# Forget attention and two MLPs: where VectorE and TensorE place the fifth attention unit and two weight packets

## The chip, the cores and the metric

The kernel runs on one core of a Trainium2 chip. The metric is device time in microseconds of one execution; smaller is better. Matrix products run on TensorE, elementwise work on VectorE, ScalarE and GpSimd, and SyncE's queue (SP) issues nearly all transfers. Each engine takes its instructions strictly in the order in which they were written for it.

## The reference

```python
q, k, v: (4, 8, 576, 64); s: (4, 8, 576)
cum = cumsum(maximum(s, 0))
scores = q @ k.T / 8 + minimum(-(cum_i - cum_j), 0), -1e9 above the diagonal
attn = softmax(scores); x = (attn @ v) as (2304, 512)
h = x @ w_in1;  x = (s * relu(h)**2 + b) @ w_out1      # 512 -> 2048 -> 512
h = x @ w_in2;  out = (relu(h) + alpha * min(h, 0)) @ w_out2
```

Inputs and outputs are float32; the weights arrive in a wider form and are converted on the chip.

## The kernel before

**Attention.** The work is cut into 32 units; a unit is a batch, a pair of heads and either the first 320 or the last 256 rows of queries. For each head of a unit, `scores` takes products of q and k on TensorE (L457 in the first eight units, L459 and L460 later), joins them with the gate bias on VectorE (L435 writes the bias, L461 joins and takes the row's extreme), takes exponentials on ScalarE (L473, which also sums the row), adds a small number and inverts the sum on VectorE (L480, L481), and multiplies by it on GpSimd (L484, the normalisation). `values` then transposes the result on TensorE (L515), copies it to SBUF (L519) and multiplies by v (L531); ScalarE copies the outcome into the block of x (L546). `transpose_qk` turns q and k on VectorE (L375). In names such as `sc0_3_0_0_1` the first digits are head and block of rows, the last three the unit. The first four units (numbers 0 to 3, called the early ones) have buffers of their own and run before any MLP work. While they do, TensorE also runs products of zeros that nobody reads (`busy`, L97).

**The MLP.** Tokens go in blocks of 256. A block needs all of its x, split by ScalarE (L130, the rounded part) and VectorE or GpSimd (L131, the rest): `xh` and `xl`, each in four pieces. The hidden layer goes in 16 slices f: `up` (L772, twelve matmuls into `hp`), relu and square on ScalarE (L791, L793), a split into `gh` and `gl` (L130, L131), and `down` (L886, twelve matmuls), which trails `up` by two slices.

**Weight packets.** Slice f of the first layer comes as packet f: two transfers of 512 KB (L208 `wi`, L212 `wo`) into raw tiles, and for each half a ScalarE pass (L140), two VectorE passes (L141, L142, after which the raw tile is free) and a split (L130 on ScalarE; L131 on VectorE for `wi`, on GpSimd for `wo`). The raw tiles are reused in a fixed rotation: packets 3 and 6 share one pair, 4 and 7 another, 5 and 8 a third.

**What sets the order.** The program is written as Python generators that take turns, and a scheduler with a model of the engines then orders each engine's instructions, preferring what was written earlier. `tc.issue_after(ins)` holds everything in its block, on the engine of `ins`, behind `ins`. The fifth unit is number 4 (`EARLY`), the first one without buffers of its own. Before the change, packets 0 to 3 and this unit's turning and first scores were written among the early units, with packet 4 (`AHEAD - 1` = 3, `AHEAD` = 4) written with the first slice:

```python
        yield from alternate(scores(us[2], 1), values(us[1], 1))
        packet(0, 3)
        yield from alternate(scores(us[3], 0), values(us[2], 0), transpose_qk(u))
```

Of the kernel before, what the change touches and what calls it, by code (L numbers as in the profile page):

```python
# [19 lines left out]
def tile_forget_attention__then__two_mlps(  # L20
# [108 lines left out]
    def split(hi, lo, src, lo_eng=nc.vector):  # L129
        nc.scalar.copy(hi, src)  # L130
        lo_eng.tensor_tensor(out=lo, in0=src, in1=hi.bitcast(F32), op=ALU.subtract)  # L131

# [123 lines left out]

    xf = {}

# [110 lines left out]
    def transpose_qk(u):  # L369
# [4 lines left out]
        for dst, src in zip(turned, u.nats):  # L374
            nc.vector.transpose(dst, src)  # L375
        yield
# [27 lines left out]
    def scores(u, h):  # L404
# [11 lines left out]
        for r in u.blocks:  # L416
            i0, i1 = IB[r]
            rows = i1 - i0
            if u.early and r != 1:
                big, col = u.buf(two, 0, F32, "", f"probs{h}{r}"), 0  # L420

            width = -(-i1 // P) * P if i1 < S else S
            pt = probs[r] = big[:, col : col + width]
            col += width
            if width > i1:
                nc.gpsimd.memset(pt[:, i1:], 0.0)
            if r == 0:
                nc.gpsimd.memset(pt[64:P, 0:64], 0.0)

            if flip:  # L430
                nc.scalar.activation(
                    pt[:rows, :i1], u.cums[h][:rows, :i1], AF.Relu, scale=-1.0, bias=cumT[:rows, r, head : head + 1]
                )
            else:
                nc.vector.tensor_scalar(  # L435
                    out=pt[:rows, :i1], in0=u.cums[h][:rows, :i1], scalar1=cumT[:rows, r, head : head + 1],
                    scalar2=0.0, op0=ALU.subtract, op1=ALU.min,
                )
            nc.gpsimd.affine_select(
                out=pt[:rows, i0:i1], in_=pt[:rows, i0:i1], pattern=[[-1, rows]], base=0,  # L440
                channel_multiplier=1, compare_op=ALU.is_ge,
                fill=-MASKED if flip else MASKED,
            )
# [36 lines left out]
        nc.vector.tensor_scalar(out=sm[:, :nr], in0=sm[:, :nr], scalar1=1e-9, scalar2=None, op0=ALU.add)  # L480
        nc.vector.reciprocal(sm[:, :nr], sm[:, :nr])  # L481
        for m, r in enumerate(u.blocks):
# [7 lines left out]
    def values(u, h):  # L490
# [45 lines left out]
        if u.n < EARLY:  # L536
            busy(4 if (u.n, h) == (EARLY - 1, 0) else 1)
        t0 = u.b * S + q0
# [22 lines left out]

    done = 0

    def attention():
# [32 lines left out]
        yield from alternate(scores(us[2], 1), values(us[1], 1))  # L597
        packet(0, 3)
        yield from alternate(scores(us[3], 0), values(us[2], 0), transpose_qk(u))
        yield from alternate(scores(us[3], 1), values(us[2], 1))  # L600
        yield from values(us[3], 0)
        last = us[3]
        for n in range(EARLY, len(units)):
            nxt = Unit(n + 1) if n + 1 < len(units) else None
            if nxt:
                load_qk(nxt)
            yield from alternate(scores(u, 0), values(last, 1))
            done = n
# [21 lines left out]
    def inputs(layer, t):  # L630
# [20 lines left out]
        for c in range(NCC):  # L651
            on_pool = layer == 0 and t
            split(xh[c], xl[c], src[:, c], nc.gpsimd if on_pool else nc.vector)
        return xh, xl
# [314 lines left out]
    while done < reached(0):  # L969
        next(side)  # L970
    for f in range(AHEAD):
        packet(0, f)
    fetch(0, AHEAD + 1)

    x, late = inputs(0, 0), []
    for n in range(len(BLOCKS) * NF):
# [5 lines left out]
        if layer == 0 and t == 0 and f + AHEAD < NF:  # L982
            with tc.issue_after(relus[f - 1]) if f else nullcontext():
                packet(0, f + AHEAD)
            for g in range(f + AHEAD + 1, min(f + AHEAD + 3, NF)):
                fetch(0, g)
# [54 lines left out]
```

## Time and profile before

| | |
|---|---|
| Median of 3 runs | 1041.17 us (1040.21 to 1043.41) |
| Profiled execution, its own time | 1043.1 us |
| Its span, first to last instruction | 1041.2 us |
| TensorE busy | 1021.4 us, 98% of the span |
| VectorE busy | 686.3 us, 66% |
| ScalarE busy | 672.7 us, 65% |
| GpSimd busy | 468.1 us, 45% |
| Mean granted TensorE clock | 0.993 of full speed |

The busy time of an engine counts instructions that do work. TensorE's matmuls overlap, so its busy time is not its peak. "Granted clock" is the share of full speed that the chip gave TensorE.

### The profile page before, as it was taken

Reading aid. Unit: us, or ns where it says so; the run is one execution under the profiler, and the core shown is the slowest. Engines: PE = TensorE matmul, PEld = TensorE weight load, DVE = VectorE, ACT = ScalarE, POOL = GpSimd, SP = SyncE. Lnnn points to the kernel's source line nnn. Section 1 sums busy time; section 2 is a strip of 40 time slices with the busy share of each in tenths; the row PEclk is TensorE's granted clock in tenths of the full one; section 3 lists DMA queues with packets and bytes.
Section 4 is the critical chain, followed back from the end, with each engine's and each line's share of the span. In section 5 each row is a group of like instructions: output and inputs, shape, how many; then the busy total and the mean of one; then the engine's idle time right before and its main releaser. Section 6 shows DMA issues by size and latency. Waiting matters only on the chain.

```text
span 1041.2 us, 20629 instructions
## 1 busy us (share of the span) xinstructions
PE 1021.4 (98%) x6952; PEld 927.0 (89%) x6952; DVE 686.3 (66%) x1605; ACT 672.7 (65%) x1669; POOL 468.1 (45%) x892
## 2 busy tenths in 40 slices
PE   9889999999999999999999999999999999999998
PEld 4568899999999999999999888998799999999996
DVE  6879875687677766667655975767775456446443
ACT  5868866777787877778776776645564455345443
POOL 5546675666677666677562100288721011001000
PEclk9889999999999999999999999999999999999999
DMA  7979533343232432234214762466654235334331
GB/s 157 268 174 252 150 63 69 69 97 72 52 84 62 90 92 52 67 68 93 64 44 145 241 201 81 124 194 200 196 178 143 98 101 179 105 95 132 107 104 55
DMA packets 197929, 125.44 MB, mean 120 GB/s; under 512 B 138496, under 2 KB 167936, under 8 KB 197824
## 3 DMA queue, kind: packets, MB, share of 16 engines
q1 hardware_dynamic: 193744, 123.56, 42.9%
q8 instruction: 55, 0.90, 0.4%
q10 hardware_dynamic: 4080, 0.57, 0.3%
q14 instruction: 50, 0.41, 0.1%
HBM read 106.19 MB, written 17.90 MB: 119 GB/s over the span
## 4 chain that ended last, share of the span: by engine, by line
PE 77%; DMA 5%; POOL 5%; ACT 4%; DVE 4%; issue 3%; SPq 1%; ACTq 0%; DVEq 0%; POOLq 0%
PE hp L772 18%; PE acc L896 16%; PE acc L886 16%; PE p L806 13%; PE pt L515 4%; PE av L531 4%; POOL sum L727 2%; PE sc L460 2%; DMA vn<-in_v_dram 1%; PE sc L459 1%; DMA sums_d<-w 1%; DMA wo<-in_moe_w_out_dram 1%; PE acc_first L97 1%; PE sc L457 1%; POOL probs L484 1%
## 5 line engine op out<-in xcount | busy, mean ns | idle before, releaser
L772 PE MATMUL hp<-xh,w 128*128 128x256 f32 (+1 forms) x1024 | 229.1, 301 | 0.5 <-ACT r L791 0.5
L896 PE MATMUL acc<-w,ring 128*128 128x512 f32 x864 | 214.1, 391 | 0.0
L896 PEld LDWEIGHTS acc<-w,ring 128*128 128x128 f32 x864 | 156.0, 188 | 27.8
L772 PEld LDWEIGHTS hp<-xh,w 128*128 128x128 f32 x1024 | 171.4, 189 | 6.6 <-ACT r L791 1.0
L886 PE MATMUL acc<-gh,w 128*128 128x256 f32 x896 | 172.3, 286 | 0.5 <-ACT res L915 0.3
L772 PE MATMUL hp<-xl,w 128*128 128x256 f32 (+1 forms) x512 | 152.6, 298 | 0.0
L886 PEld LDWEIGHTS acc<-gh,w 128*128 128x128 f32 x896 | 136.0, 189 | 3.1 <-issue 1.6
L872 POOL TENSOR_TENSOR cc<-u,t 128x256 f32<-128x256 f32 x32 | 25.9, 809 | 228.9 <-DVE u L863 198.9
L886 PE MATMUL acc<-gl,w 128*128 128x256 f32 x448 | 118.7, 288 | 2.0 <-POOL gl L131 2.0
L484 POOL TENSOR_SCALAR probs<-probs,sm 64x64 f32<-64x64 f32 (+4 forms) x160 | 91.0, 581 | 64.8 <-DVE sm L481 52.5
L473 ACT ACTIVATE probs<-probs,nm 64x64 f32<-64x64 f32 (+4 forms) x160 | 90.0, 563 | 37.8 <-DVE nm L461 25.7
L131 POOL TENSOR_TENSOR gl<-r,gh 128x256 fp32r<-128x256 f32 x112 | 89.3, 797 | 51.3 <-ACT gh L130 44.8
L806 PE MATMUL p<-xs,sums 128*128 128x256 f32 x768 | 104.4, 282 | 0.7 <-DVE u L848 0.7
L806 PEld LDWEIGHTS p<-xs,sums 128*128 128x128 f32 x768 | 97.8, 189 | 2.8 <-DVE u L848 1.2
L772 PEld LDWEIGHTS hp<-xl,w 128*128 128x128 f32 x512 | 97.1, 190 | 3.3 <-issue 0.4
L461 DVE CUSTOM_DVE_ANT_0 probs<-sc,probs 128x320 f32<-128x320 f32 (+3 forms) x160 | 68.2, 427 | 40.4 <-PE sc L460 28.0
L791 ACT ACTIVATE r<-hp 128x256 f32<-128x256 f32 (+1 forms) x144 | 58.1, 403 | 44.5 <-PE hp L772 36.9
L806 PEld LDWEIGHTS p<-xs,w 128*128 128x128 f32 x576 | 78.8, 189 | 9.0 <-DVE u L863 2.3
L806 PE MATMUL p<-xs,w 128*128 128x256 f32 x576 | 82.2, 283 | 2.4 <-DVE u L863 1.5
L886 PEld LDWEIGHTS acc<-gl,w 128*128 128x128 f32 x448 | 80.1, 189 | 4.8 <-POOL gl L131 2.6
L515 PE MATMUL pt<-ident,probs 128*128 128x128 f32 x480 | 75.0, 277 | 5.7 <-POOL probs L484 5.6
L817 DVE SCALAR_TENSOR_TENSOR ph<-pl,misc,ph 128x512 f32<-128x512 f32 x64 | 52.7, 823 | 38.2 <-ACT pl L833 38.0
(149 smaller groups left out, 2133.9 us busy)
## 6 DMA issues: line engine op xcount, KB each, us to landing
sums<-sums_d SPq DMA_DIRECT2D x128, 256.0 KB, 2.7
wi<-in_moe_w_in_dram SPq DMA_DIRECT2D x32, 512.0 KB, 5.0
wo<-in_moe_w_out_dram SPq DMA_DIRECT2D x32, 512.0 KB, 5.0
cum<-cum_d SPq DMA_DIRECT2D x32, 288.0 KB, 3.8
sums_d<-w SPq DMA_DIRECT2D x64, 128.0 KB, 1.9
cum<-cum_d SPq DMA_DIRECT2D x30, 160.0 KB, 3.2
nat<-in_k_dram SPq DMA_DIRECT2D x64, 72.0 KB, 2.5
x_d<-res SPq DMA_DIRECT2D x18, 256.0 KB, 2.2
```

Source lines behind the costliest of these rows:

```text
L131: lo_eng.tensor_tensor(out=lo, in0=src, in1=hi.bitcast(F32), op=ALU.subtract)
L461: nc.vector.tensor_tensor_reduce(out=pt[:rows, j0:j1], in0=scr, in1=pt[:rows, j0:j1], scale=SCALE if flip else -SCALE, scalar=init, op0=AL ...
L473: nc.scalar.activation(pt[:rows, :n], pt[:rows, :n], AF.Exp, bias=nm[:rows, m : m + 1], scale=1.0 if flip else -1.0, accum_out=sm[:rows, m ...
L484: nc.gpsimd.tensor_scalar(out=probs[r][:rows, :n], in0=probs[r][:rows, :n], scalar1=sm[:rows, m : m + 1], scalar2=1.0, op0=ALU.mult, op1=A ...
L515: nc.tensor.transpose(tp[:, o : o + P], u.probs[h][r][:, k0 : k0 + P], ident)
L531: nc.tensor.matmul(av[:, nq - w : nq], lhs, part[:, o : o + w], start=(c == 0 and z == 0), stop=(c == last_c and z == len(parts) - 1), ski ...
L772: nc.tensor.matmul(hs, a[:, c], b[c], start=(n == 0), stop=(n == len(terms) * NCC - 1))
L791: relus.append(nc.scalar.activation(r, hs, AF.Relu, scale=1.0 / W_SCALE).ins)
L806: nc.tensor.matmul(bank, lhs[:, c * P : (c + 1) * P], rhs[:, c], start=(start and c == 0 and z == 0), stop=(c == 1 and z == 2), skip_group ...
L817: nc.vector.scalar_tensor_tensor(out=r, in0=u, scalar=nalpha[:, f : f + 1], in1=r, op0=ALU.mult, op1=ALU.add).ins
L886: nc.tensor.matmul(banks[d] if count == 2 else acc[d // 2][:, d % 2], a[:, d * P : (d + 1) * P], b, start=(f == 0 and (d % 2 == 0 or count ...
L896: nc.tensor.matmul(banks[m], a[:, m * P : (m + 1) * P], b, start=(f == 0 and b is woh and a is gh), stop=(f == NF - 1 and a is gl),)
```

## The change

The turning and the biases of unit 4 on VectorE are held behind the eighth reciprocal (L481), which is that of the last early head (`turns[2 * EARLY - 1]`). Packet 3 is held behind the fourth `xl` split of the first block, on VectorE (`x_parts[-1]`), and so is packet 4. The last `values` of the early units is written before unit 4's scores, so that the block of x is complete first. Four products of zeros after the first head of unit 3 become one. All arithmetic stays.

```diff
-        return
+    def behind_early(u):
+        return tc.issue_after(turns[2 * EARLY - 1]) if u.n == EARLY else nullcontext()
...
         for dst, src in zip(turned, u.nats):
-            nc.vector.transpose(dst, src)
+            with behind_early(u):
+                nc.vector.transpose(dst, src)
...
-                nc.vector.tensor_scalar(
+                with behind_early(u):
+                    nc.vector.tensor_scalar(
...
-        nc.vector.reciprocal(sm[:, :nr], sm[:, :nr])
+        turns.append(nc.vector.reciprocal(sm[:, :nr], sm[:, :nr]).ins)
...
-            busy(4 if (u.n, h) == (EARLY - 1, 0) else 1)
+            busy(1)
...
-        packet(0, 3)
-        yield from alternate(scores(us[3], 0), values(us[2], 0), transpose_qk(u))
+        yield from alternate(scores(us[3], 0), values(us[2], 0))
         yield from alternate(scores(us[3], 1), values(us[2], 1))
         yield from values(us[3], 0)
+        yield from alternate(values(us[3], 1), transpose_qk(u))
+        done = EARLY
+        yield
...
-            yield from alternate(scores(u, 0), values(last, 1))
+            yield from alternate(scores(u, 0), *([values(last, 1)] if n > EARLY else []))
...
-            split(xh[c], xl[c], src[:, c], nc.gpsimd if on_pool else nc.vector)
+            x_parts.append(split(xh[c], xl[c], src[:, c], nc.gpsimd if on_pool else nc.vector))
...
-    for f in range(AHEAD):
-        packet(0, f)
+    x, late = inputs(0, 0), []
+    with tc.issue_after(x_parts[-1]):
+        packet(0, AHEAD - 1)
     fetch(0, AHEAD + 1)
...
-            with tc.issue_after(relus[f - 1]) if f else nullcontext():
+            with tc.issue_after(relus[f - 1] if f else x_parts[-1]):
                 packet(0, f + AHEAD)
```

On VectorE, before: the sum and the reciprocal of unit 3's second head (`sm_3_0_1`) among packets 3 and 4 (`wt_3`, `wt_4`) and the turning and biases of unit 4 (`turned_0_1`, `probs_0_1_0`).

```order
L470 TENSOR_SCALAR nm_3_0_1_722<-nm_3_0_1_722 128x1
L141 TENSOR_SCALAR wt_4_0_901<-wt_4_0_901 128x512
L131 TENSOR_TENSOR xl_0_870<-xf_433,xh_0_869 128x256
L142 SCALAR_TENSOR_TENSOR wt_4_0_901<-wi_4_272,wt_4_0_901 128x512
L375 STREAM_TRANSPOSE turned_0_1_695<-nat_0_1_564 128x832
L131 TENSOR_TENSOR w_3_0_11_654<-wt_3_0_645,w_3_0_12_653 128x512
L435 TENSOR_SCALAR probs_0_1_0_817<-cum_0_0_1_573,cumT 128x448
L435 TENSOR_SCALAR probs_0_1_0_817<-cum_0_0_1_573,cumT 128x576
L141 TENSOR_SCALAR wt_4_1_905<-wt_4_1_905 128x512
L480 TENSOR_SCALAR sm_3_0_1_723<-sm_3_0_1_723 128x3
L142 SCALAR_TENSOR_TENSOR wt_4_1_905<-wo_4_273,wt_4_1_905 128x512
L481 RECIPROCAL sm_3_0_1_723<-sm_3_0_1_723 128x3
```

The same place in the changed kernel, where lines stand a few numbers later (L472 for L470, L482 for L480, L483 for L481, L376 for L375, L437 for L435):

```order
L472 TENSOR_SCALAR nm_3_0_1_704<-nm_3_0_1_704 128x1
L131 TENSOR_TENSOR xl_0_807<-xf_433,xh_0_806 128x256
L482 TENSOR_SCALAR sm_3_0_1_705<-sm_3_0_1_705 128x3
L483 RECIPROCAL sm_3_0_1_705<-sm_3_0_1_705 128x3
L376 STREAM_TRANSPOSE turned_0_1_794<-nat_0_1_564 128x832
L437 TENSOR_SCALAR probs_0_1_0_889<-cum_0_0_1_573,cumT 128x448
L437 TENSOR_SCALAR probs_0_1_0_889<-cum_0_0_1_573,cumT 128x576
```

The sum and the reciprocal now follow one `xl` split; packets 3 and 4 are gone from here, and the turning and the biases stand behind the reciprocal.

On VectorE in the changed kernel, from the fourth `xl` split on; before, nothing of packets 3 and 4 stood behind that split.

```order
L131 TENSOR_TENSOR xl_0_807<-xf_433,xh_0_806 128x256
L141 TENSOR_SCALAR wt_3_0_816<-wt_3_0_816 128x512
L141 TENSOR_SCALAR wt_3_1_820<-wt_3_1_820 128x512
L141 TENSOR_SCALAR wt_4_0_858<-wt_4_0_858 128x512
L141 TENSOR_SCALAR wt_4_1_862<-wt_4_1_862 128x512
L463 ISA probs_0_1_1_920,nm_0_1_1_918<-sc_4_0_0_0_1_943,probs_0_1_1_920 128x320
L463 ISA nm_0_1_1_918 128x1
L142 SCALAR_TENSOR_TENSOR wt_3_0_816<-wi_3_262,wt_3_0_816 128x512
L376 STREAM_TRANSPOSE turned_1_1_916<-nat_1_1_878 128x832
L142 SCALAR_TENSOR_TENSOR wt_3_1_820<-wo_3_263,wt_3_1_820 128x512
L142 SCALAR_TENSOR_TENSOR wt_4_0_858<-wi_4_272,wt_4_0_858 128x512
L142 SCALAR_TENSOR_TENSOR wt_4_1_862<-wo_4_273,wt_4_1_862 128x512
```

Both packets' VectorE passes have come here, behind the block's x and mixed with unit 4's second head and unit 5's turning.

On ScalarE, before: from the relu of slice 1 (`r_1`) to its rounded part `gh_0_1`, on which `down` of slice 1 waits.

```order
L791 ACTIVATE r_1_1181<-hp_0_1_1166 128x256
L140 ACTIVATE wt_6_0_1226<-wi_6_917 128x512
L140 ACTIVATE wt_6_1_1230<-wo_6_918 128x512
L130 CAST w_5_2_22_1198<-wt_5_1_1190 128x512
L793 ACTIVATE r_1_1181<-r_1_1181 128x256
...
L130 CAST gh_0_1_1179<-r_1_1181 128x256
```

And in the changed kernel:

```order
L798 ACTIVATE r_1_1178<-hp_0_1_1163 128x256
L130 CAST w_4_0_16_866<-wt_4_0_858 128x512
L140 ACTIVATE wt_6_0_1223<-wi_6_874 128x512
L130 CAST w_4_2_18_870<-wt_4_1_862 128x512
L800 ACTIVATE r_1_1178<-r_1_1178 128x256
L140 ACTIVATE wt_6_1_1227<-wo_6_875 128x512
L130 CAST gh_0_1_1176<-r_1_1178 128x256
```

The split of packet 4 has come in between, and the passes over packet 6 stand ahead of `gh_0_1` as before; packet 6 is fetched into the raw tiles that packet 3 leaves.

## Rows read from the trace of the kernel before

**Rows 1.** The page: each engine's busy time over the span.
```profile
PE 1021.4 (98%) x6952; PEld 927.0 (89%) x6952; DVE 686.3 (66%) x1605; ACT 672.7 (65%) x1669; POOL 468.1 (45%) x892
```
**Rows 2.** Windows: stretch: length, busy of PE, PEld, DVE, ACT, POOL, clock, DMA, GB/s.
```profile
52.00:54.00 2.00, 0.91 (x4) 0.37 (x2) 2.00 (x4) 0.83 (x3) 2.00 (x4) 0.85 1.08 397
54.00:56.00 2.00, 0.30 (x2) 0.30 (x3) 2.00 (x7) 1.15 (x3) 1.89 (x4) 0.50 1.09 333
...
53.80:60.70 6.90, 5.00 (x17) 3.41 (x18) 4.20 (x14) 3.14 (x9) 5.09 (x8) 0.54 0.94 181
```
**Rows 3.** Timeline of TensorE: start, length, what, [idle before <- releaser].
```profile
45.66 1.30 PE L531 MATMUL acc_first<-pf,vn 128*128 128x320 f32 x6
46.79 1.03 PE L97 MATMUL acc_first<-dense 128*128 128x512 bf16 x4
48.26 0.55 PE L515 MATMUL pt<-ident,probs 128*128 128x128 f32 x3 [0.43 <-POOL probs L484]
...
50.96 1.96 PE L457 MATMUL sc<-turned 64*128 64x448 f32 x6 [0.58 <-DVE turned L375]
55.70 0.90 PE L515 MATMUL pt<-ident,probs 128*128 128x128 f32 x3 [2.79 <-POOL probs L484]
...
64.13 0.47 PE L772 MATMUL hp<-xh,w 128*128 128x256 f32 x1
```
**Rows 4.** Timeline of VectorE, same columns.
```profile
49.78 1.03 DVE L375 STREAM_TRANSPOSE turned<-nat 128x832 f32<-128x832 f32 x1
...
53.11 0.51 DVE L141 TENSOR_SCALAR wt<-wt 128x512 uint32<-128x512 uint32 x1
53.54 0.25 DVE L480 TENSOR_SCALAR sm<-sm 128x3 f32<-128x3 f32 x1
53.70 0.68 DVE L142 SCALAR_TENSOR_TENSOR wt<-wo,wt 128x512 uint32<-128x512 uint32 x1
54.30 0.16 DVE L481 RECIPROCAL sm<-sm 128x3 f32<-128x3 f32 x1
54.39 0.68 DVE L131 TENSOR_TENSOR w<-wt,w 128x512 fp32r<-128x512 f32 x1
...
65.92 0.51 DVE L131 TENSOR_TENSOR xl<-xf,xh 128x256 fp32r<-128x256 f32 x1 [0.56 <-ACT xh L130]
```
**Rows 5.** Timeline of ScalarE: the row sum of unit 3's second head.
```profile
49.02 0.19 ACT L473 ACTIVATION_READ_ACCUMULATOR probs<-probs,nm 128x1 f32 x1
```
**Rows 6.** Timeline of GpSimd: normalisations of unit 3's two heads.
```profile
45.66 0.40 POOL L484 TENSOR_SCALAR probs<-probs,sm 64x64 f32<-64x64 f32 x1 [2.50 <-DVE sm L481]
...
54.64 1.52 POOL L484 TENSOR_SCALAR probs<-probs,sm 64x64 f32<-64x64 f32 x3
```
**Rows 7.** VectorE's groups from 64 to 132 us: busy, mean ns | idle before.
```profile
L141 DVE TENSOR_SCALAR wt<-wt 128x512 uint32<-128x512 uint32 x21 | 14.4, 691 | 2.7 <-ACT wt L140 2.6
L142 DVE SCALAR_TENSOR_TENSOR wt<-wi,wt 128x512 uint32<-128x512 uint32 x11 | 11.7, 1060 | 0.2
L131 DVE TENSOR_TENSOR w<-wt,w 128x512 fp32r<-128x512 f32 x11 | 8.6, 786 | 1.9 <-POOL sm L413 1.9
L142 DVE SCALAR_TENSOR_TENSOR wt<-wo,wt 128x512 uint32<-128x512 uint32 x10 | 8.0, 795 | 0.1
```
**Rows 8.** Timeline of TensorE: attention of units 4 and 5, spacing of matmuls.
```profile
61.80 1.24 PE L457 MATMUL sc<-turned 64*128 64x320 f32 x4
...
65.38 1.04 PE L515 MATMUL pt<-ident,probs 128*128 128x128 f32 x8
...
66.84 1.02 PE L531 MATMUL av<-pf,vn 128*128 128x256 f32 x4
...
68.27 1.02 PE L457 MATMUL sc<-turned 64*128 64x448 f32 x2
...
71.58 1.09 PE L531 MATMUL av<-pf,vn 128*128 128x256 f32 x6
...
76.08 0.28 PE L772 MATMUL hp<-xh,w 128*128 128x256 f32 x1
76.20 0.27 PE L772 MATMUL hp<-xl,w 128*128 128x256 f32 x1
```
**Rows 9.** Tile `wo`, 20 to 140 us: issue to landing of packets' second halves.
```profile
DMA to landing us min/median/max: 3.6/5.6/8.8
```
**Rows 10.** Windows, columns as in rows 2: the first block.
```profile
64.10:131.60 67.50, 66.20 (x432) 55.28 (x432) 60.23 (x119) 56.18 (x133) 43.68 (x59) 1.00 0.70 179
```

More of the change, by code (lines that the diff above doesn't have):

```diff
@@ L130, in split @@
         nc.scalar.copy(hi, src)
-        lo_eng.tensor_tensor(out=lo, in0=src, in1=hi.bitcast(F32), op=ALU.subtract)
+        return lo_eng.tensor_tensor(out=lo, in0=src, in1=hi.bitcast(F32), op=ALU.subtract).ins
     def convert(raw, wt):
@@ L255, in sum_columns @@
             )
-    xf = {}
+    xf, x_parts = {}, []
     def x_block(t):
@@ L434, in scores @@
             else:
-                nc.vector.tensor_scalar(
-                    out=pt[:rows, :i1], in0=u.cums[h][:rows, :i1], scalar1=cumT[:rows, r, head : head + 1],
-                    scalar2=0.0, op0=ALU.subtract, op1=ALU.min,
-                )
+                with behind_early(u):
+                    nc.vector.tensor_scalar(
+                        out=pt[:rows, :i1], in0=u.cums[h][:rows, :i1], scalar1=cumT[:rows, r, head : head + 1],
+                        scalar2=0.0, op0=ALU.subtract, op1=ALU.min,
+                    )
             nc.gpsimd.affine_select(
@@ L560, in alternate @@
                     gens.remove(g)
-    done = 0
+    done, turns = 0, []
+    def behind_early(u):
+        return tc.issue_after(turns[2 * EARLY - 1]) if u.n == EARLY else nullcontext()
     def attention():
@@ L970, in tile_forget_attention__then__two_mlps @@
         next(side)
-    for f in range(AHEAD):
-        packet(0, f)
+    x, late = inputs(0, 0), []
+    with tc.issue_after(x_parts[-1]):
+        packet(0, AHEAD - 1)
     fetch(0, AHEAD + 1)
-    x, late = inputs(0, 0), []
     for n in range(len(BLOCKS) * NF):
```

## The prediction, made before the changed kernel ran

> **What bounds the kernel now.** I began with the busy times: TensorE works 98% of the span, and no other engine is above 66% [rows 1]. So the time can fall only where TensorE waits, runs at a lower clock, or does work that nobody needs, and whatever is gained early reaches the end as long as TensorE stays the bound. Then I looked for such places with the windows of two microseconds. The worst lies just ahead of the first MLP block: from 54 to 56 us TensorE is busy 0.30 of 2.00 us, and the granted clock is 0.50 [rows 2]. The timeline of TensorE says what it waits for: the transposes at 55.70 come after 2.79 us of idleness, released by GpSimd's normalisation [rows 3]. That normalisation starts at 54.64 [rows 6], right after the reciprocal at 54.30, and the sum ahead of the reciprocal starts at 53.54 [rows 4]. But ScalarE had delivered the row sum at 49.02 + 0.19 = 49.21 [rows 5]. For 4.3 us a ready result stood in VectorE's queue behind packets 3 and 4 and unit 4's turning and biases, as the order before shows. This is what the change moves. The first block's first matmul starts at 64.13 [rows 3].
>
> **The change, part by part.** Four terms.
>
> First, the waits. In the new order only one `xl` split stands ahead of the sum and the reciprocal, so the normalisation of the last early head should come near 48 us, when TensorE does not need it yet. The 2.79 us go. So do 0.58 us ahead of 50.96, where TensorE waited for unit 4's turning [rows 3]: packets no longer stand in front of it, and in TensorE's new order unit 4's scores come after more of the early products. The 0.43 us ahead of 48.26 [rows 3] change shape. TensorE's new order puts the transposes of unit 3's first head before the products that start at 45.66 [rows 3]. With the packet passes gone, its reciprocal should be ready about half a microsecond earlier, and the normalisation, now started at about 45.0 instead of 45.66 and 1.52 us long [rows 6], ends at about 46.5; TensorE is free at 45.66, so it waits about 0.8 us. Sum: 2.79 + 0.58 + 0.43 - 0.8 = 3.0 us gained.
>
> Second, the clock. From 53.80 to 60.70 TensorE is busy 5.00 us at a granted clock of 0.54 [rows 2], that is nearly all at 1.2 GHz, the lower level; the fall followed the idle stretch above (0.91 busy of 2.00 from 52 to 54). At 2.4 GHz the same work takes half: 2.5 us gained, if no new idle stretch of that size takes the old one's place. From 44 us on I find only the 0.8 us above.
>
> Third, the products of zeros. Four took 1.03 us at full clock [rows 3]; three go: 3 x 1.03 / 4 = 0.8 us.
>
> So TensorE should be 6.3 us ahead when the first block starts. Two score products of unit 4's second head now stand behind that start; four of that length took 1.24 us [rows 8]. They only change places, but the first block's first matmul should show at about 64.1 - 6.3 - 1.2 = 56.6 us.
>
> Fourth, what the packets cost in their new place. Each needs two L141, two L142 and one L131 on VectorE. By the durations near 53 us [rows 4] that is 2 x 0.51 + 2 x 0.68 + 0.68 = 3.1 us, 6.1 us for both; by the means in the first block [rows 7] 2 x 0.69 + 1.06 + 0.80 + 0.79 = 4.0, 8.1 us for both. The Trainium skill, page "GPSIMD Engine Reference", section Specifications, says that GpSimd's SBUF interfaces are shared with VectorE and that VectorE instructions with two SBUF inputs contend there. L142 and L131 have two such inputs, and the trace agrees: 0.68 us near 53 against means of 1.06 and 0.80 in rows 7. By that rule the pair would cost 8.1 us, without it 6.1.
>
> How much of this TensorE feels depends on who waits. The chain I find longest runs through the raw tiles. Before, the fourth `xl` split ended 2.3 us after the block's start (65.92 + 0.51 against 64.13 [rows 3, 4]); so now near 58.9. Behind it stand four L141 (2.0), a score step (0.6), L142 of packet 3's first half (0.7), a turning (1.0) and L142 of its second half (0.7): the second raw tile is free at 63.9. The fetch of packet 6's second half goes there; with the issue (0.4, an estimate) and a landing of 5.6 us [rows 9] it is in SBUF at 69.9. ScalarE then does L140 and the rounding `gh` of slice 1, which in its new order stands right behind: about 1.1 us, so 71.0. TensorE wants that `gh` for `down` of slice 1. Before it there stand three `up` and one `down`, 48 matmuls at 0.12 us [rows 8] = 5.8 us, and five pieces of unit 4's and unit 5's attention, 1.24 + 1.04 + 1.02 + 1.02 + 1.09 = 5.4 us [rows 8], about 4.7 where the tail of each, some 0.15, lies beside the next (an estimate): TensorE arrives at 56.6 + 10.5 = 67.1, or near 67.9 with the small waits that this stretch also had before. It waits 3.1 us. The weights of slice 3, the other candidate, are then ready too: from the split at 58.9, the 12 to 13 us of VectorE work in front of them end at about 71.5. So both reach TensorE together, and I count the delay once: 3.1 us lost. The bounds: nothing, if the landing is short and TensorE slower; and 8.1 us, if both packets at the higher price stand wholly in TensorE's way. I take the value of the chain, as its pieces are rows.
>
> ScalarE's and GpSimd's parts of the packets move too (four L140 stay early, four casts and two GpSimd splits go later). SP's queue holds packet 6 back, as counted; unit 5's and unit 6's transfers pass it. I cost these at nothing more, since in the first block ScalarE is busy 56.18 of 67.50 us and GpSimd 43.68 [rows 10]; if that cover fails, it fails in the way of the fourth rival.
>
> Sum: 3.0 + 2.5 + 0.8 - 3.1 = 3.2 us gained. The sum is made on the profiled execution: 1043.1 - 3.2 = 1039.9 us. That execution was 1.9 us above the median, and I carry the gain to the median: 1041.2 - 3.2 = **1038.0 us**. A difference of 0.3%, 3.1 us, is about what a measurement of this kernel can tell from none.
>
> **The rivals.** With the landing of 3.6 or 8.8 us in place of 5.6 [rows 9], the likeliest case runs from 1036.0 to 1041.2.
>
> *The packets hide completely.* The first three terms stand and the fourth is nothing: 1041.2 - 6.3 = 1034.9. For it speaks that TensorE had packets 0 to 2 ready and attention work to fill with; against it, that its order is fixed and `down` of slice 1 cannot be passed over.
>
> *The clock falls again.* A wait of over 3 us inside the first block is as long as the one after which the clock fell before (2.79 [rows 3]). A half-rate stretch of the same length costs up to 6.9 / 2 = 3.4 us, and the net is 3.2 - 3.4: 1041.4. Against it: unlike then, TensorE would be dense on both sides of the wait. The Trainium skill, page "TensorE: Matmul & The Clock Gate", section on HAM oscillation, describes this: waits for transfers inside a loop let the clock fall again and again. The trace agrees for one such wait only, that of rows 2.
>
> *VectorE becomes the bound: slower.* From 64.10 to 131.60 VectorE is busy 60.23 of 67.50 us [rows 10], so 7.3 idle. Now 8.1 us of packets and about 1.0 us of unit 4's score steps come on top: 69.3 us. Starting 6.3 us earlier and idling as much, it ends at 57.8 + 69.3 + 7.3 = 134.4, 2.9 us later than before, and the attention that the second block waits for comes as much later: 1044.1. It decides from the point where VectorE's idle time in this stretch stays above 4.4 us. Against it: TensorE was busy 66.20 of those 67.50 us, so VectorE's idle time there was waiting that a longer queue can fill.
>
> *The change doesn't reach TensorE.* Unit 4's q, k and v land late, or the transposes of unit 3 wait for another step on ScalarE, and the gap moves by a microsecond instead of closing: about 1041. The reciprocal's place in the order speaks against it.
>
> **How the numbers follow.** Likeliest case 0.40, half of it beyond 0.3%; complete hiding 0.22; the clock 0.13; VectorE 0.17; no effect 0.08. Faster by over 0.3%: 0.20 + 0.22 + 0.03 = 0.45. Slower: 0.17 + 0.01 = 0.18. Within: 0.37. The range runs from a little below complete hiding, 1034.6, to 1043.0, where the fourth term has its upper bound (1041.2 - 6.3 + 8.1 = 1043.0); beyond lie most of the VectorE case and a tail below.
>
> **What would show it.** In the new profile the first block's first matmul should start near 56.6 us; no idle of over 1 us should stand ahead of unit 3's transposes; the clock should show one half-rate stretch (36 to 44 us) and no second; a wait of some 3 us should stand on `down` of slice 1 or `up` of slice 3, near 68 to 72 us. If the block starts at 60 or later, the first two terms are wrong; if it starts near 57 and the end has not moved, the fourth is, and VectorE's idle time up to unit 8's turning will say which rival it was.

## The result, and the profile after

| | before | after |
|---|---|---|
| Median | 1041.45 us (6 runs, 1040.21 to 1043.53) | 1049.98 us (6 runs, 1048.29 to 1057.60) |
| Ratio to before | | 1.0101 (95%: 1.0077 to 1.0125) |
| Profiled execution: time, span, clock | 1043.1, 1041.2, 0.993 | 1048.66, 1046.9, 0.991 |

The change makes the kernel about 1% slower: 1.0101 is the recorded ratio with its interval, the two medians by themselves give 1.0082, 8.5 us. The prediction was 1038.0 us, range 1034.6 to 1043.0: wrong in direction and outside its range.

The gap ahead of the first block is gone. First the page's busy times, then the windows of [rows 2] (same columns), the first matmul of the block and the reciprocal of unit 3's second head from the timelines, all of the changed kernel:

```profile
PE 1023.8 (98%) x6949; PEld 929.4 (89%) x6949; DVE 681.3 (65%) x1605; ACT 672.5 (64%) x1669; POOL 469.8 (45%) x892
```
```profile
52.00:54.00 2.00, 2.00 (x12) 1.26 (x11) 1.34 (x6) 1.50 (x5) 0.00 (x0) 1.00 1.31 174
54.00:56.00 2.00, 2.00 (x11) 1.33 (x10) 0.92 (x5) 1.55 (x4) 0.32 (x1) 1.00 0.67 102
53.80:60.70 6.90, 6.90 (x39) 5.20 (x39) 4.44 (x14) 4.33 (x12) 1.51 (x3) 1.00 0.46 114
```
```profile
47.52 0.18 DVE L483 RECIPROCAL sm<-sm 128x3 f32<-128x3 f32 x1
55.65 0.47 PE L779 MATMUL hp<-xh,w 128*128 128x256 f32 x1
```

The reciprocal comes 6.8 us earlier, TensorE is busy all the time at full clock, and the block starts at 55.65 in place of 64.13 [rows 3]. These 8.5 us are lost again further on, and 5.7 us more: the span is 1046.9 us in place of 1041.2. Most of this shows between 60 and 170 us, as idle time of TensorE and as low clock. The window, before and then after (columns as in [rows 2]):

```profile
60.00:170.00 110.00, 108.50 (x726) 93.87 (x725) 85.80 (x202) 82.27 (x206) 69.80 (x121) 1.00 0.57 140
```
```profile
60.00:170.00 110.00, 101.57 (x645) 87.64 (x644) 86.68 (x191) 77.27 (x192) 71.81 (x119) 0.95 0.57 148
```

TensorE is idle for 1.5 us of these 110 before and for 8.4 after, and a clock of 0.95 in place of 1.00 costs some 5 us (an estimate: 0.05 x 110). The three longest waits, from its timeline, and windows around two of them:

```profile
68.46 0.73 PE L893 MATMUL acc<-gh,w 128*128 128x256 f32 x4 [1.31 <-ACT gh L130]
93.79 1.86 PE L459 MATMUL sc<-turned 64*128 64x448 f32 x2 [2.34 <-DVE turned L376]
154.15 0.51 PE L893 MATMUL acc<-gh,w 128*128 128x256 f32 x2 [2.10 <-ACT w L130]
```
```profile
93.00:100.50 7.50, 6.71 (x20) 4.98 (x21) 7.50 (x16) 5.17 (x12) 5.25 (x6) 0.55 0.77 182
120.00:130.00 10.00, 10.00 (x66) 8.33 (x65) 5.20 (x14) 4.18 (x13) 5.82 (x9) 1.00 0.29 54
130.00:140.00 10.00, 10.00 (x64) 8.03 (x63) 4.55 (x16) 6.09 (x15) 4.01 (x10) 1.00 0.22 45
150.00:160.00 10.00, 7.90 (x47) 7.56 (x46) 7.53 (x25) 7.31 (x20) 9.17 (x22) 0.83 0.35 79
```

TensorE's order holds unit 6's score products right behind a slice of the MLP; they wait 2.34 us for unit 6's turning, and the clock is at 0.55 around them. It is low again behind the wait of 2.10 us, where `down` of the last slice needs packet 15's second half. That half goes through a tile of its own, `last`, which takes turns in its buffers with the attention's copies (L520, L524 of the changed kernel), and its passes stand among late attention work in ScalarE's order, 8.2 us later than before. ScalarE's timeline before, then after:

```profile
141.61 0.67 ACT L140 ACTIVATE last<-wo 128x512 f32<-128x512 f32 x1
```
```profile
149.81 0.68 ACT L140 ACTIVATE last<-wo 128x512 f32<-128x512 f32 x1
```

The turnings tell how far the attention has come. VectorE's timeline before (units 6, 7, 8), then after:

```profile
83.00 1.03 DVE L375 STREAM_TRANSPOSE turned<-nat 128x832 f32<-128x832 f32 x1
105.26 1.03 DVE L375 STREAM_TRANSPOSE turned<-nat 128x832 f32<-128x832 f32 x1
131.64 0.83 DVE L375 STREAM_TRANSPOSE turned<-nat 128x640 f32<-128x640 f32 x1
```
```profile
92.69 1.04 DVE L376 STREAM_TRANSPOSE turned<-nat 128x832 f32<-128x832 f32 x1
122.33 1.03 DVE L376 STREAM_TRANSPOSE turned<-nat 128x832 f32<-128x832 f32 x1
138.68 0.85 DVE L376 STREAM_TRANSPOSE turned<-nat 128x640 f32<-128x640 f32 x1
```

The MLP starts 8.5 us earlier, and the attention beside it runs 9.7, 17.1 and 7.0 us later. VectorE's passes on the packets' tile `wt` alone (windows: length, VectorE's busy time, clock, DMA, GB/s), before and then after:

```profile
44.00:58.00 14.00, 7.00 (x10) 0.84 1.09 285
58.00:126.00 68.00, 37.96 (x49) 0.98 0.71 182
```
```profile
44.00:58.00 14.00, 0.48 (x2) 1.00 0.92 221
58.00:126.00 68.00, 46.28 (x62) 0.95 0.70 197
```

From 58 to 126 us VectorE does 13 more packet passes, 8.3 us. The same windows with the work of all engines are, of the changed kernel,

```profile
44.00:58.00 14.00, 13.86 (x72) 9.50 (x70) 8.85 (x33) 10.07 (x30) 6.39 (x14) 1.00 0.92 221
58.00:126.00 68.00, 61.91 (x390) 51.85 (x388) 62.73 (x117) 51.29 (x119) 44.58 (x52) 0.95 0.70 197
```

and of the kernel before

```profile
44.00:58.00 14.00, 10.20 (x46) 6.81 (x45) 13.83 (x37) 10.29 (x26) 9.32 (x13) 0.84 1.09 285
58.00:126.00 68.00, 66.70 (x412) 53.82 (x412) 58.79 (x124) 53.02 (x125) 40.27 (x55) 0.98 0.71 182
```

From 58 us on that is 3.9 us more, so 4.4 us of other work, nearly all of it the attention's, were pushed behind 126 us.

### The profile page after: what moved, and what is told of

It reads as the page before. It is cut to its first block, busy times and chain, and to the rows that moved or that the text cites. A ratio compares the mean times of both kernels' runs of the same rounds, so it can differ in the third digit from the quotient of the medians.

```text
span 1046.9 us, 20604 instructions
## 1 busy us (share of the span) xinstructions
PE 1023.8 (98%) x6949; PEld 929.4 (89%) x6949; DVE 681.3 (65%) x1605; ACT 672.5 (64%) x1669; POOL 469.8 (45%) x892
## 4 chain that ended last, share of the span: by engine, by line
PE 82%; DVE 5%; DMA 4%; POOL 3%; ACT 2%; issue 2%; ACTq 0%; SPq 0%; DVEq 0%; POOLq 0%
PE hp L779 19%; PE acc L893 18%; PE acc L903 16%; PE p L813 13%; PE av L533 5%; PE pt L517 4%; PE sc L462 2%; PE sc L459 2%; POOL sum L734 2%; PE sc L461 2%; DMA wo<-in_moe_w_out_dram 1%; DMA sums_d<-w 1%; DVE w L131 1%; DMA cum<-cum_d 1%; PE colsum L245 1%
## 5 line engine op out<-in xcount | busy, mean ns | idle before, releaser
L131 POOL TENSOR_TENSOR gl<-r,gh 128x256 fp32r<-128x256 f32 x112 | 89.3, 797 | 64.3 <-ACT gh L130 57.9
L475 ACT ACTIVATE probs<-probs,nm 128x448 f32<-128x448 f32 (+4 forms) x160 | 89.9, 562 | 39.3 <-DVE nm L463 25.2
```

What stands on the lines that cost most here:

```text
L131: return lo_eng.tensor_tensor(out=lo, in0=src, in1=hi.bitcast(F32), op=ALU.subtract).ins
L475: nc.scalar.activation(pt[:rows, :n], pt[:rows, :n], AF.Exp, bias=nm[:rows, m : m + 1], scale=1.0 if flip else -1.0, accum_out=sm[:rows, m ...
```

## The experiments

The scheduler places instructions by a simulated timeline (`schedule_with_timeline_sim=True`), so an edit can make a new order for the whole block. The passes counted here are the last 75 that VectorE makes on the packets' tile `wt` in the first layer: 73 of packets 1 to 15 and two of packet 0's, since the second half of packet 15 goes through `last`. The table has, for the kernels that were compared most, how many of these the order places ahead of the turnings of units 6 and 7, the start of the turnings of units 6, 7 and 8 in the trace, and TensorE's idle time from 60 to 170 us.

| kernel | passes ahead, 6 / 7 | turnings at (us) | idle, 60 to 170 (us) | ratio to before |
|---|---|---|---|---|
| before | 36 / 53 | 83.0, 105.3, 131.6 | 1.5 | 1 |
| e18 | 40 / 57 | 83.3, 105.8, 129.9 | 2.8 | 1.0015 |
| e2 | 41 / 62 | 85.2, 109.0, 130.8 | 5.9 | 0.9999 |
| e12 | 42 / 61 | 84.1, 106.5, 127.4 | 1.5 | 1.0007 |
| e1 | 38 / 65 | 90.9, 120.6, 140.9 | 6.7 | 1.0080 |
| e11 | 48 / 67 | 89.0, 112.3, 133.1 | 7.7 | 1.0051 |
| e4 | 48 / 71 | 88.4, 115.3, 133.1 | 9.8 | 1.0070 |
| e17 | 48 / 71 | 91.1, 119.2, 137.3 | 8.9 | 1.0075 |
| e5 | 48 / 73 | 95.2, 122.9, 139.6 | 9.2 | 1.0065 |
| after | 49 / 75 | 92.7, 122.3, 138.7 | 8.4 | 1.0101 |
| e8 (forced) | 37 / 52 | 87.9, 115.1, 142.6 | 11.0 | 1.0137 |

Over all the kernels of the study, those that lost 0.5% or more idle there for 6.6 to 11.9 us, the others for 1.5 to 5.9. The turnings are a weaker sign: e14, below, has them at 80.4, 101.5 and 125.9 us, all earlier than before, and loses 0.48%; it idles 1.9 us in this stretch, so its loss lies elsewhere.

### e1 and e2: the two parts alone

```diff
 # e1, against the changed kernel
+        packet(0, 3)
         yield from alternate(scores(us[3], 0), values(us[2], 0))
...
+    for f in range(AHEAD):
+        packet(0, f)
+    fetch(0, AHEAD + 1)
     x, late = inputs(0, 0), []
-    with tc.issue_after(x_parts[-1]):
-        packet(0, AHEAD - 1)
-    fetch(0, AHEAD + 1)
...
-            with tc.issue_after(relus[f - 1] if f else x_parts[-1]):
+            with tc.issue_after(relus[f - 1]) if f else nullcontext():
```


> Edit: the change without its packet part; packets 3, 4 and 5 stand where they stood before, ahead of the first block's x, while unit 4's turning and biases stay held behind unit 3's second reciprocal and the early products keep their new order. Theory A (the loss comes from VectorE's order further on: with packets 3 and 4 late, the passes of packets 5 to 10 come to stand ahead of unit 6's turning, TensorE waits for it 2.3 us in order and then runs some 7 us at half rate): here unit 6's turning stands behind packet 7 and parts of 8 only, as before, so no wait of over 1 us on unit 6's score products and no half-rate stretch near 95 to 102 us; the reciprocal is freed of the 2.4 us of unit 4 only, so a wait of up to 1 us stays ahead of unit 3's transposes; 1035 to 1040 us. Theory B (VectorE's sum of work from 56 to 132 us is the bound, in whatever order): the same work on VectorE, the time near the changed kernel's, 1047 to 1051. Theory C (the new order of unit 4's attention costs the time, since attention trails): 1047 to 1051 too, with the packets innocent.

Measured: 1050.67 us, ratio 1.0080 (1.0051 to 1.0109). The wait of up to 1 us ahead of unit 3's transposes that was expected is 3.82 us, more than before, and the first block starts at 66.11:

```profile
55.10 0.47 PE L517 MATMUL pt<-ident,probs 128*128 128x128 f32 x1 [3.82 <-POOL probs L486]
```

```diff
 # e2, against the kernel before
...
-        packet(0, 3)
...
-    for f in range(AHEAD):
-        packet(0, f)
+    x, late = inputs(0, 0), []
+    with tc.issue_after(x_parts[-1]):
+        packet(0, AHEAD - 1)
...
-            with tc.issue_after(relus[f - 1]) if f else nullcontext():
+            with tc.issue_after(relus[f - 1] if f else x_parts[-1]):
```

> Edit: the change without its attention part; packets 3, 4 and 5 go behind the first block's x, unit 4's turning, biases and scores stand as before. Theory A: the reciprocal is freed of the packets' 5 to 6 us, so the wait of 2.8 us ahead of unit 3's transposes goes nearly wholly, with the half-rate stretch behind it; but unit 6's turning comes behind all of packet 8, so a wait of 0.5 to 2 us on unit 6's first score products with part of the half-rate stretch: 1040 to 1049 us. Theory B: as the changed kernel, 1047 to 1051. Theory C (attention's order is what costs): 1034 to 1038.

Measured: 1040.80 us, ratio 0.9999 (0.9980 to 1.0018). Theory A said that the packets' place costs and unit 4's hold gains; neither came. The packets alone cost and gain nothing over the whole run: TensorE idles 3.2 us up to 60 us in place of 7.4, and 5.9 in place of 1.5 from there to 170. The rest of the change alone costs 0.8%, but in part where the changed kernel has no wait, and much of it goes with the clock: e1's two executions with a granted clock of 0.996 took 1042.4 and 1042.8 us.

### e3: unit 6's turning ahead of packet 10

```diff
...
-                packet(0, f + AHEAD)
+                with tc.issue_after(turning[EARLY + 2]) if f + AHEAD == 10 else nullcontext():
+                    packet(0, f + AHEAD)
```


> Edit: the changed kernel, with packet 10 held behind unit 6's turning in the order; nothing else. In VectorE's order the turning then stands ahead of four passes of packet 10 that stood before it, 3.6 us by the changed kernel's trace. Theory A: the wait of 2.34 us on unit 6's first score products goes, and the half-rate stretch from 95 to 102 us with it (3.4 us): 1044 to 1046 us, a gain of 4 to 6 against the changed kernel. Theory B (VectorE's throughput bounds): the four passes only come later, packet 10 becomes what TensorE waits for, and the time stays at 1048 to 1051. Theory C (attention trails): a gain of 2.3 us at most, 1047 to 1050.

Measured: 1052.73 us, ratio 1.0112 (1.0071 to 1.0153). The 2.34 us are gone, but 2.47 stand on `gh` further on, and the idle time from 60 to 170 us is 10.2 us: taking one wait away did not take away the loss. Theory A falls.

```profile
109.17 0.92 PE L893 MATMUL acc<-gh,w 128*128 128x256 f32 x4 [2.47 <-ACT gh L130]
```

### e4 to e7: the pieces of the attention part

```diff
 # e4
-        yield from values(us[3], 0)
-        yield from alternate(values(us[3], 1), transpose_qk(u))
-        done = EARLY
-        yield
+        yield from alternate(values(us[3], 0), transpose_qk(u))
...
-            yield from alternate(scores(u, 0), *([values(last, 1)] if n > EARLY else []))
+            yield from alternate(scores(u, 0), values(last, 1))
 # e5, and the same at the biases
-            with behind_early(u):
-                nc.vector.transpose(dst, src)
+            nc.vector.transpose(dst, src)
 # e6
-            busy(1)
+            busy(4 if (u.n, h) == (EARLY - 1, 0) else 1)
 # e7
-        done = EARLY
-        yield
```

> Edit: the changed kernel with the attention in the order of before: unit 4's first scores run beside the second product of unit 3 again, and the first block's x and the packets come after them; only unit 4's turning and biases stay held behind unit 3's second reciprocal, and packets 3 to 5 behind x. The run with the packets alone moved stood level with the kernel before, the run with unit 4 alone moved lost 1%. Theory H (the hold costs it): still 1047 to 1051 us. Theory O (the new order of the attention steps, with x and the packets ahead of unit 4's scores, costs it): 1038 to 1042. Theory L (what costs is how many packet passes stand ahead of unit 6's and unit 7's turning on VectorE, whichever edit put them there; in this kernel's order it is 12 and 18 more than before): 1046 to 1050.

Measured: 1046.72 us, ratio 1.0070 (1.0049 to 1.0091).

> Edit: the changed kernel without the hold of unit 4's turning and biases behind the reciprocal; packets and the attention order as changed. Theory H: 1038 to 1042 us. Theory O: 1047 to 1051. Theory L (12 and 20 more packet passes ahead of unit 6's and unit 7's turning than before): 1046 to 1050.

Measured: 1046.48 us, ratio 1.0065 (1.0045 to 1.0085).

> Edit: the changed kernel with four products of zeros behind unit 3's last product, as before, in place of one. If the three products kept the clock up across the start of the first block: 1043 to 1047 us and a granted clock near 0.996 over the run. If they are work that nobody needs, as the prediction counted them: 0.8 us more than the changed kernel, 1048 to 1052, at the same clock.

Measured: 1051.96 us, ratio 1.0118 (1.0099 to 1.0138), median clock 0.993. The four products do not rescue the changed kernel.

> Edit: the changed kernel without the two lines that let the first block's x and packets be issued ahead of unit 4's first scores; products of unit 3's second head ahead of unit 4, hold and packets as changed. Theory O, if it is this place of x that costs: 1038 to 1042 us. Theory H: 1047 to 1051. Theory L (13 and 22 more packet passes ahead of unit 6's and unit 7's turning than before, as in the changed kernel): 1047 to 1051.

Measured: 1050.97 us, ratio 1.0101 (1.0074 to 1.0128). The loss stays without the order (e4) and without the hold (e5), so neither H nor O fits both; L fits them and e7. That the hold or the order costs anything by itself isn't shown: e4 and e5 share the packets' place and the one product of zeros, and e17 below, with these two alone, loses as much.

### e8 to e10: fewer packet passes ahead, by force

```diff
...
-                packet(0, f + AHEAD)
+                n_turn = EARLY + 3 if f + AHEAD >= 11 else EARLY + 2
+                with tc.issue_after(turning[n_turn]) if f + AHEAD >= 8 else nullcontext():
+                    packet(0, f + AHEAD)
```


> Edit: the changed kernel, with packets 8 to 15 held behind unit 6's turning and packets 11 to 15 also behind unit 7's. In VectorE's order 37 and 52 of the 75 packet passes of packets 1 to 15 then stand ahead of the two turnings, as in the kernel before (36 and 53); in the changed kernel it is 49 and 75. Theory L (those passes, which the sum of the change's edits let overtake the attention, are what costs): the loss goes, 1034 to 1041 us, level with the kernel before or up to 6 us better, as the first block still starts 8 us earlier. Theory V (VectorE's sum of work in the first block bounds, in whatever order): TensorE waits for packets in place of turnings, 1046 to 1051.

Measured: 1053.57 us, ratio 1.0137 (1.0122 to 1.0152). TensorE now waits for packet 11, which the edit holds behind unit 7's turning:

```profile
126.56 0.80 PE L779 MATMUL hp<-xh,w 128*128 128x256 f32 x2 [4.03 <-DVE w L131]
```

The same holds in the order on e2 (e9) and on e4 (e10):

> Edit: the kernel with the packets alone moved (level with the kernel before; 41 and 62 passes ahead of the two turnings), with the same holds, so 37 and 52. Theory L: some gain, 1034 to 1039 us. Theory V: 1040 to 1046, what the earlier start gives is taken back as in the kernel without the holds.

Measured: 1049.44 us, ratio 1.0080 (1.0052 to 1.0108).

> Edit: the kernel of the changed holds with the attention in the order of before (1046.7 us; 48 and 71 passes ahead of the two turnings), with the same two holds added, so 37 and 52. Theory L: 1034 to 1041 us. Theory V: 1045 to 1049.

Measured: 1048.45 us, ratio 1.0084 (1.0067 to 1.0101). So the counts are no lever by themselves: L, as a cause, falls. They may be a sign of an order in which the MLP runs ahead. Forced down, waits on the packets' passes on VectorE come up: 4.0 us in e8, 2.0 in e10, 0.7 in e9. The ratio of e9 mixes two kinds of executions, 1043.1 and 1043.7 us at clocks of 0.998 and 0.994 and three of 1049.4 to 1049.7 at 0.987, so most of its loss goes with the clock.

### e11 and e12: the packets into VectorE's idle time

```diff
-    with tc.issue_after(x_parts[-1]):
+    with tc.issue_after(turns[2 * EARLY - 1]):
         packet(0, AHEAD - 1)
```
(and the same for packet 4; e11 in the changed kernel, e12 in e2.)

> Edit: the changed kernel, but packets 3 to 5 are held behind unit 3's second reciprocal, as unit 4's turning is, and no longer behind the first block's x. Theory V (VectorE paces the first block: in the changed kernel it stands idle for 5.2 of the 14 us from 44 to 58 us, where the kernel before had it busy for 13.8, and the work that is missing there stands in the way of TensorE from 58 to 126 us): the packets fill that idle time, VectorE is busy over 11 of those 14 us, the later waits shrink, 1041 to 1046 us. Theory S (which instruction the order places ahead of which turning decides, not the amount of work; here 48 and 67 packet passes stand ahead of the turnings of units 6 and 7, nearly as in the changed kernel): 1047 to 1052.

Measured: 1045.29 us, ratio 1.0051 (1.0031 to 1.0071), in theory V's range and below theory S's. VectorE is busy 11.68 of the 14 us, as V expected:

```profile
44.00:58.00 14.00, 13.38 (x60) 9.03 (x58) 11.68 (x31) 10.64 (x30) 6.00 (x9) 0.89 0.83 193
```

> Edit: the kernel with the packets alone moved (level with the kernel before), but the packets held behind unit 3's second reciprocal in place of x; unit 4 as before. Theory V: VectorE busy over 11 of the 14 us from 44 to 58 (9.3 in the kernel with the packets behind x), 1034 to 1039 us, the best of all. Theory S (42 and 61 passes ahead of the turnings, against 41 and 62): 1039 to 1042, as with the packets behind x.

Measured: 1041.36 us, ratio 1.0007 (0.9985 to 1.0030), no gain over e2, though the first block starts at 55.24. Here theory S is right and V, which expected the best kernel of all, wrong.

### e13 to e16: load taken off VectorE

```diff
-... nc.gpsimd if layer == 0 and n else nc.vector)
+... nc.gpsimd if layer == 0 and (n or f in (5, 7, 9, 11)) else nc.vector)
```
in after (e13), before (e14), e11 (e15) and e12 (e16).

> Edit: the changed kernel, with the first-half split of packets 5, 7, 9 and 11 on GpSimd in place of VectorE. In the changed kernel's trace 13 such splits take VectorE 11.7 us from 58 to 126 us, so four are 3.6 us of 62.7; on GpSimd, busy 44.6 of 68 there, four at 1.47 are 5.9 us. Theory V (VectorE's load in that stretch is what TensorE waits for, through the attention that falls behind): 1043 to 1047 us. Theory S (the place of single instructions in the order decides, the load does not): 1048 to 1052.

Measured: 1053.07 us, ratio 1.0126 (1.0109 to 1.0143). GpSimd became what TensorE waits for:

```profile
104.70 0.58 PE L893 MATMUL acc<-gl,w 128*128 128x256 f32 x1 [3.05 <-POOL gl L131]
```

> Edit: the kernel before, with the same four splits on GpSimd. VectorE is busy 58.8 of 68 us from 58 to 126 there, so theory V expects little: 1038 to 1041 us. Theory S: 1039 to 1043, no change or a loss by GpSimd's slower pass.

Measured: 1044.37 us, ratio 1.0048 (1.0032 to 1.0063).

> Edit: the kernel with unit 4 and the packets both behind unit 3's reciprocal (1045.3 us), with the same four splits on GpSimd. Theory V: 1040 to 1044 us. Theory S: 1044 to 1048.

Measured: 1047.47 us, ratio 1.0071 (1.0052 to 1.0091).

> Edit: the kernel with the packets alone behind the reciprocal (1041.4 us), with the same four splits on GpSimd. Theory V: 1036 to 1040 us, which would beat the kernel before. Theory S: 1040 to 1044.

Measured: 1042.79 us, ratio 1.0036 (1.0018 to 1.0054). None gained, as theory V wanted in three; e15 and e16 lie in theory S's ranges, e13 and e14 1.1 and 1.4 us above them. The test is not clean, since the work went to an engine that TensorE waits for too.

### e17 and e18: three products of zeros

```diff
-            busy(4 if (u.n, h) == (EARLY - 1, 0) else 1)
+            busy(1)
```
in e2 (e17) and in the kernel before (e18), and nothing else.

> Edit: the kernel with the packets alone moved (level with the kernel before), with one product of zeros behind unit 3's last product in place of four; not one line of unit 4 or of the packets differs. Theory P (the prediction's third term: three products of nobody's work go): 0.8 us less, 1039 to 1041 us. Theory S (the order that the scheduler makes for the whole first block follows from such small shifts: here 48 and 71 of the 75 packet passes stand ahead of the turnings of units 6 and 7, against 41 and 62 with four products, and just as in the kernel with the hold alone, 1046.7 us): 1044 to 1049 us.

Measured: 1050.38 us, ratio 1.0075 (1.0055 to 1.0096).

> Edit: the kernel before, with one product of zeros behind unit 3's last product in place of four, and nothing else. Theory P: 0.8 us less, 1038.5 to 1040.5 us. Theory S: here 40 and 57 packet passes stand ahead of the turnings of units 6 and 7, against 36 and 53; fewer than in the slow kernels, so 1040 to 1044.

Measured: 1042.75 us, ratio 1.0015 (1.0003 to 1.0028).

e18 lies in theory S's range, e17 1.4 us above it, and both are slower than theory P allows. With the packets late, taking out three products that took 0.8 us costs 0.75%; e2 with all four had lost nothing. Windows of e2, then of e17 (columns as in [rows 2]):

```profile
44.00:58.00 14.00, 13.87 (x68) 8.98 (x68) 9.33 (x34) 9.08 (x26) 6.30 (x14) 1.00 0.87 189
58.00:126.00 68.00, 64.25 (x415) 54.53 (x413) 62.61 (x123) 53.31 (x126) 48.39 (x54) 0.97 0.71 211
```
```profile
44.00:58.00 14.00, 13.86 (x72) 9.52 (x72) 8.71 (x32) 10.39 (x31) 6.30 (x14) 1.00 0.97 203
58.00:126.00 68.00, 61.66 (x373) 51.70 (x371) 63.03 (x123) 51.22 (x119) 43.54 (x52) 0.92 0.75 205
```

VectorE is about as busy in both; TensorE has 42 matmuls fewer done from 58 to 126 us in e17. That the products themselves kept TensorE faster is unlikely, since e6, which has them back in the changed kernel with the same 49 and 75 passes ahead, did not gain. What differs is the order: 48 and 71 passes ahead in place of 41 and 62, turnings 6 to 10 us later, and a wait of 3.50 us:

```profile
104.48 0.47 PE L515 MATMUL pt<-ident,probs 128*128 128x128 f32 x1 [3.50 <-POOL probs L484]
```

No kernel of the study beats the one before.

## Why the prediction was wrong, point by point

**First term, the waits (3.0 us): right, a little small.** From 44 to 58 us TensorE is idle 0.1 us in place of 3.8, since the wait of 0.8 us that was reckoned with did not come. The block was to start near 56.6 us and started at 55.65, with no idle time ahead of unit 3's transposes.

**Second term, the clock (2.5 us): right in the trace, but taken from one execution.** Over 19 runs beside e1 to e3 the kernel before had a median granted clock of 0.996; the profiled execution had 0.993, 0.3% or 3.1 us lower. The fall behind the wait of 2.79 us varies. In e14 and e18 a wait of that length stands there too (e18's timeline and then its windows):

```profile
54.83 0.55 PE L515 MATMUL pt<-ident,probs 128*128 128x128 f32 x3 [2.79 <-POOL probs L484]
```
```profile
54.00:56.00 2.00, 1.17 (x6) 0.90 (x7) 1.82 (x9) 1.24 (x5) 2.00 (x5) 0.89 1.05 367
56.00:58.00 2.00, 2.00 (x9) 1.56 (x7) 1.13 (x2) 1.34 (x5) 0.77 (x1) 0.50 1.37 170
58.00:60.00 2.00, 2.00 (x5) 0.96 (x5) 0.62 (x3) 0.57 (x1) 1.34 (x2) 0.75 0.64 61
```

By these rows the clock took at most 2 x (0.11 + 0.50 + 0.25) = 1.7 us, where before it stayed at about half speed from 53.80 to 60.70 [rows 2].

**Third term, three zero products (0.8 us gained): wrong in sign.** e18 puts it at a loss of 0.15%, e17 at 0.75% once the packets are late. I priced the instruction and not the order that follows from its absence.

**Fourth term, the packets (3.1 us lost): right in place and chain, too large in size, and wrong as the end of the account.** The wait on `down` of slice 1 came where it was expected, at 68.46, at 1.31 us, within the bounds. The chain was the reckoned one, only earlier: packet 6's second half, reckoned in SBUF at 69.9, was there by 67.45, and `gh` followed right behind it.

```profile
67.45 0.66 ACT L140 ACTIVATE wt<-wo 128x512 f32<-128x512 f32 x1 [2.08 <-DMA wo<-in_moe_w_out_dram]
```

But e2 shows the packets alone at nothing net, so the first two terms' gain was given back there too, and the change's loss comes later.

The packets' ten passes themselves took 6.0 us on VectorE, near the lower of the two prices. But the rows behind the two prices don't set VectorE with GpSimd against VectorE without it: the 0.68 us near 53 fell beside a GpSimd that was busy 2.00 of 2.00 us from 52 to 54 [rows 2], with the mask (L439). Beside its split (L131) and the start of a normalisation the same pass took 1.66 us, in the kernel before:

```profile
46.34 1.66 DVE L142 SCALAR_TENSOR_TENSOR wt<-wo,wt 128x512 uint32<-128x512 uint32 x1
```
```profile
46.03 1.26 POOL L131 TENSOR_TENSOR w<-wt,w 128x512 fp32r<-128x512 f32 x1
...
52.83 1.70 POOL L439 TENSOR_SCALAR_AFFINE_SELECT probs<-probs 128x128 f32<-128x128 f32 x3
```

**The step that failed** is the sum itself: four terms up to some 70 us, with everything behind taken as unchanged but earlier, on the premise that what is gained early reaches the end as long as TensorE stays the bound. Waits and low clock further on stood at nothing in it; only the rivals had them. What came in their place is 6.9 us more idle time of TensorE from 60 to 170 us (8.4 against 1.5), of which the fourth term's wait is 1.31, and two stretches at half the clock. The order was new up to the end of the first block: 49 and 75 passes ahead of the turnings of units 6 and 7, against 36 and 53. Its rows could be read before the run, and I compared them only around the moved instructions.

**The rivals.** "VectorE becomes the bound" had the right sign, and its marker came: unit 8's turning is 7.0 us late (it said 2.9). That its time, 1044.1 us, is passed by 5.9 us shows that it was not all. Its mechanism holds in part. Around 93 to 100.5 us VectorE is full (7.50 of 7.50, above), but up to unit 8's turning it is not:

```profile
55.65:138.68 83.03, 76.94 (x483) 64.19 (x482) 67.76 (x136) 60.34 (x144) 51.48 (x66) 0.96 0.63 175
```

It is busy 67.76 us (reckoned: 69.3) and idle 15.3 (reckoned: 7.3). The packets come first, and then VectorE is busy only 9.75 us of the 20 from 120 to 140; that it waits there for the attention's chain, which goes from engine to engine, is argued and not shown. "The clock falls again" came true too, at other waits than the one it was made for: 0.55 from 93.0 to 100.5 us, 0.83 from 150 to 160, and none behind the 1.31 us. The Trainium skill, page "TensorE: Matmul & The Clock Gate", section on HAM oscillation, describes such repeated falls behind waits for transfers in a loop; this trace now shows two, behind waits for VectorE and for ScalarE. The median clock of the changed kernel's six runs is 0.991, 0.5% under 0.996: an estimate from these two gives the clock up to 5 of the 8.5 us. In the two profiled executions (0.993 and 0.991) it has a smaller part: TensorE is busy 2.4 us longer (1023.8 against 1021.4) and idle 3.3 us longer.

What stays open is which feature of these orders makes TensorE wait, and what the scheduler's own timeline gave for them; no run compared the two.

## What to carry to other kernels

Where a scheduler makes the order from simulated times, even a small edit can re-make the order of all that follows (e17); compare the whole order, and above all how two interleaved streams (here the packets' passes and the attention's turnings) stand to each other, before summing local gains. An earlier start of one stream need not gain anything while the stream beside it keeps or loses its pace (e2 and e12 here). And set a clock loss seen in one profiled execution against the time of the other executions before counting it as a gain.

## What the runs showed of the hardware

The granted clock differs between executions of one kernel, and their times with it, by as much as the effects studied here: e1's ten runs lie from 1042.4 us at a clock of 0.996 to 1052.4 at 0.987, and 19 of the kernel before from 1037.9 at 0.998 to 1046.8 at 0.989. A wait of 2.79 us stands at the same place in three traces: before, the clock was 0.54 over the 6.90 us from 53.80 on [rows 2]; in e14 and e18 it was 0.75 over the same stretch. Behind a wait of 3.82 us (e1) low clock lasted longer: the rows are its windows.

```profile
56.00:58.00 2.00, 2.00 (x4) 0.67 (x3) 1.24 (x4) 0.00 (x0) 2.00 (x3) 0.50 1.08 376
58.00:64.00 6.00, 6.00 (x16) 3.75 (x16) 1.81 (x9) 2.69 (x7) 1.17 (x3) 0.50 0.86 140
```

The length of a wait alone doesn't say whether the clock falls. Behind the 1.31 us at 68.46 in the changed kernel it stayed at 1.00 (64 to 75 us); in e17, behind a wait of 1.08 us ahead of 75.58, it was 0.52 from 77.0 to 80.5 us.

In these traces a VectorE pass over a packet takes longer beside some of GpSimd's work. In the kernel before, up to 160 us, eleven L142 with nothing on GpSimd beside them took 0.68 to 0.69 us each, three that ran mostly beside its normalisation (L484) 1.02 on the mean, and eight mostly beside its split (L131) 1.40. L141, which reads one tensor and not two, took 0.42 alone and 0.96 beside the split.
